# Pass 1 of an FFT and soft-MoE kernel: the last batch turned ahead of the remaining T, late T copies split between ScalarE and VectorE

## The chip, the core and the metric

One NeuronCore of a Trainium2 chip runs the whole program. The metric is device time in microseconds (us). Engines are named as in the profile: PE (TensorE, matrix multiply), PEld (its weight loads), DVE (VectorE), ACT (ScalarE), POOL (GpSimd), SP (SyncE, which issues nearly all DMAs).

## What is computed

```python
X = np.fft.fft(np.fft.fft(x, axis=1), axis=2).real   # x: 8 x 3072 x 256
x = X.reshape(24576, 256)
logits = x @ phi                                     # 32 slots
d = softmax over tokens;  c = softmax over slots
slot_out = experts(d.T @ x)                          # relu MLP, 8 experts
y = c @ slot_out
out = (s * relu(y @ w_in)**2 + b) @ w_out
```

The FFT is never formed. Pass 1, where the change lies, projects `x` on `phi` after a transform along the feature axis (folded into a small table `phd`), and then does the first of two steps of the transform along the sequence. Its result is the table `tt`, from which the next stage ("lp") makes the logits.

## The kernel before, in words

**Pass 1** (lines 357 to 481) has eight batches of three 1 MB pages of `x` each. A batch has two parts, so there are sixteen numbers n = 2b + part, and three kinds of step:

- V(n), `emit_v` (L371): matmuls (L383) of the pages of a part into the PSUM tile `vt`; part 0 needs the first two pages of its batch, part 1 the third. ScalarE copies `vt` to `vts` (L392).
- turn(n), `turn_v` (L394): TensorE transposes `vts` into `vq` (L401; four transposes in part 0, three in part 1). A copy (L405) takes `vq` to `v`; a planner's counter for each engine decides whether ScalarE or VectorE does it.
- T(b, h), `emit_t` (L413): for each half h of a batch four calls make 16 small matmuls (L422; 32 in the trace, where an f32 matmul has two records) into one PSUM tile `tps`, of which there are four buffers. The fourth call issues eight copies (L435) of the tile to `tt`, on ScalarE, or all eight on VectorE. T(b, .) needs the `v` of both parts of batch b.

The loop (L455) goes V(n), half a T (of the batch before), turn(n - 1). After the last V it runs T(6, 1), turn(15), and then, behind the last DMA issues of the pass, T(7, 0) and T(7, 1).

The program order of every engine is the order in which the Python code issues instructions. **The planner** (`at`, L107) is a set of counters, in us, for TensorE, ScalarE, VectorE and the DMA. `busy` adds a cost to a counter. `fill` (L138) issues steps of side work as long as VectorE's counter is not ahead of TensorE's. The side work of this pass is the loading, decoding and splitting of `w_out`: four loads of 1 MB (`raw`, L148), a chain on VectorE for each (L152 to L172, L198), at the end a maximum over partitions on TensorE (`mx`, L233 and L238), eight products on VectorE (L259), each with a cast on ScalarE (L261) and a subtraction on POOL (L262), and one matmul `bp` (L272) with its product on VectorE (L273). `pump_a` issues the loads in the order of a string (L289), in which the pages of `x` (x) and the loads of `w_out` (w) alternate; the first four pages go ahead of it. The third w lies between the two pages of part 0 of batch 4, the fourth between them and the third page of batch 5.

Behind pass 1, at L489 to L492, ScalarE fills a small constant `stack` with six instructions; its first use is much later (L815). Then comes the lp stage (L518): matmuls of `tt` with a table (L526), copies to `lg` on ScalarE (L539), maxima on VectorE (L541), a global maximum (L545 to L562), and then exponentials (L623). Much later the loads of `w2` (L762) go into pages that the experts' matmuls (L852) free.

Of the kernel before, what the change touches and what calls it, by code (L numbers as in the profile page):

```python
# [32 lines left out]
def tile_fft2__then__softmoe__then__act_relu2(  # L33
# [18 lines left out]
    nc = tc.nc  # L52
    P = 128
    NS1 = 24
    B, S, D = 8, NS1 * P, xp.shape[-1]
# [24 lines left out]
    ident = const.tile([P, P], F32, name="ident")  # L80
# [18 lines left out]
    def free_pages(among=9):  # L99
        return sum(max(p[1] - p[2], 0) for p in pools[:among])  # L100

    def drop(k):
        pools[k][2] -= 1

    todo = []
    side_work = []
# [7 lines left out]
    def busy(eng, cost, after=0.0):  # L114
        at[eng] = max(at[eng], after, at["pe"]) + cost
# [22 lines left out]
    def fill():  # L138
        while side_step(at["pe"] + 0.7):
            pass  # L140
# [44 lines left out]
    def keep_warm(t, k):  # L185

        for _ in range(k):
            nc.tensor.matmul(t, lhsT=ones[:, :t.shape[0]], rhs=ones[:, :t.shape[1]], start=True, stop=True)
# [117 lines left out]
    def pump_a():  # L306

        while order and at["dma"] < at["pe"] + LEAD and free_pages() >= (doubles[0][0] if order[0] == "w" else 1):
            order_step()

    x_at, pend_t, xr = [], [], []
# [33 lines left out]
    def htab_clear(i):  # L345
        for q in range(2):
            nc.gpsimd.memset(htabs[i][0][64 * q:64 * q + M, :, 1 - q], 0.0)
# [9 lines left out]
    with tc.tile_pool(name="xtp", bufs=1, side="right") as xtp, tc.tile_pool(name="vp", bufs=1, side="right") as vp, \  # L357
            tc.tile_pool(name="ps_v", bufs=1, space=PSUM) as psv:
        mxp[:] = [psv, 4]
        vs = [vp.tile([P, NE, NG * NR], F32, name=f"v{k}") for k in range(2)]  # L360
        for v in vs:
            nc.gpsimd.memset(v.rearrange("p e (b k) -> p e b k", b=NG)[:, :, :, NU:NR], 0.0)
        vts = {}

        def turned(n, c, i, k, rev):

            v = xa[n][0][:, c, i, P - 1:P] if rev else xa[n][0][:, c, i, 0:1]
            sg = -1 if rev else 1
            return bass.AP(tensor=v.tensor, offset=v.offset, ap=[list(v.ap[0]), [sg * 2 * P, k], [sg, P]])

        def emit_v(n):  # L371
            b, part = divmod(n, 2)
            x0, x2, x1 = 3 * b, 3 * b + 1, 3 * b + 2
            vt = psv.tile([P, 4, P], F32, name="vt", bufs=2)

            if part == 0:
                todo_v = [(0, 0, 0, x0, 0, 4, 0), (1, 0, 0, x0, 1, 4, 0), (0, 1, 1, x2, 6, 3, 1), (1, 1, 0, x2, 7, 4, 1)]
            else:
                todo_v = [(0, 0, 0, x1, 0, 3, 0), (1, 0, 0, x1, 1, 3, 0), (0, 1, 0, x2, 0, 1, 1), (1, 1, 0, x1, 7, 2, 1),
                          (0, 1, 1, x1, 6, 1, 1)]  # L380
            for c in range(2):
                for m, (h, sg, o, pg, i, k, rev) in enumerate(todo_v):
                    nc.tensor.matmul(vt[64 * h:64 * h + 64, o:o + k, :], lhsT=phd[:, c, sg, :],  # L383
                                     rhs=turned(pg, c, i, k, rev), start=(c == 0 and m < 2), stop=(c == 1 and m >= len(todo_v) - 2),
                                     tile_position=(0, 64 * h), skip_group_check=True)
            at["pe"] = max(at["pe"], x_at[x1 if part else x2]) + (2.3 if part else 3.6)
            for pg in ((x1, x2) if part else (x0,)):
                drop(xa[pg][1])
            busy("act", 0.5)
            ns = 3 if part else 4  # L390
            vts[n] = xtp.tile([P, 4, P], F32, name="vts", bufs=2)
            nc.scalar.copy(vts[n][:, 0:ns], vt[:, 0:ns])  # L392

        def turn_v(n):  # L394
            b, part = divmod(n, 2)
            bg, bq = divmod(b, NG)
            ns, nk = ((4, 16), (3, 10))[part]
            vq = psv.tile([P, 4, P], F32, name="vq", bufs=2)
            t = vts.pop(n)
            for si in range(ns):  # L400
                nc.tensor.transpose(vq[:, si, :], t[:, si, :], ident)  # L401
            at["pe"] += 0.44
            eng = "act" if at["act"] < at["dve"] + TOL else "dve"
            busy(eng, 0.65)
            (nc.scalar.copy if eng == "act" else nc.vector.tensor_copy)(  # L405
                vs[bg][:, :, NR * bq + 16 * part:NR * bq + 16 * part + nk],
                vq.rearrange("p s (k e) -> p e (s k)", e=NE)[:, :, 0:nk])
            if part:
                pend_t.extend((b, h) for h in range(2))

        part = []

        def emit_t():  # L413


            b, h = pend_t[0]
            bg, bq = divmod(b, NG)
            if not part:
                part[:] = [psv.tile([P, 4, P], F32, tag="tps", name="tps", bufs=4), 0]
            t, k = part  # L420
            for j in range(4):
                nc.tensor.matmul(t[32 * j:32 * j + 32, k, :], lhsT=vs[bg][:, 8 * j + 4 * h + k, NR * bq:NR * bq + NR],  # L422
                                 rhs=f_sb, start=True, stop=True, tile_position=(0, 32 * j), skip_group_check=True)
            at["pe"] += 0.3
            part[1] += 1
            if k < 3:
                return
            part.clear()
            pend_t.pop(0)
            eng = "dve" if h and not (side_work and b < B - 2) else "act"  # L430
            busy(eng, 3.4 if eng == "dve" else 3.0)
            for j in range(4):
                for c in range(2):
                    r = 64 * bg + NR * c
                    (nc.scalar.copy if eng == "act" else nc.vector.tensor_copy)(  # L435
                        tt[r:r + NR, :, bq, 8 * j + 4 * h:8 * j + 4 * h + 4],
                        t[NR * j:NR * j + NR, :, 64 * c:64 * c + 64].rearrange("p e k -> p k e"))

        def project():
            pp = psv.tile([P, 2, 2, NE], F32, tag="tps", name="pp", bufs=4)  # L440
            for j in range(2):
                for c in range(2):
                    for k in range(2):
                        nc.tensor.matmul(
                            pp[:, c, j, :], lhsT=dd[:, j, k, c * P:(c + 1) * P], rhs=phi_sb[:, k, :],
                            start=(k == 0), stop=(k == 1),
                        )
            for sg in range(2):
                nc.vector.tensor_copy(phd[:, :, sg], pp.rearrange("p c j e -> p c (j e)"))
            nc.vector.tensor_scalar(out=phd[:, :, 1, NE:], in0=pp[:, :, 1], scalar1=-1.0, scalar2=None, op0=ALU.mult)  # L450

        keep_warm(psv.tile([P, 4 * P], F32, tag="vt", name="warm", bufs=2)[:, :P], 7)
        project()
        NV = 2 * B
        for n in range(NV + 1):  # L455
            if n < NV:
                emit_v(n)
                pump_a()
                fill()
            if n == 3:  # L460
                tp = psv.tile([P, P], F32, tag="tps", name="tp", bufs=4)
                nc.tensor.transpose(tp, f_sb, ident)
                nc.vector.tensor_copy(ft_sb, tp)
            for _ in range(4):
                if pend_t:
                    emit_t()
            if n >= 1:
                turn_v(n - 1)
            fill()
            pump_a()  # L470
        while order:
            order_step()
        for _ in range(4):
            load_xr()
        while pend_t:
            emit_t()
        fill()
        for i in range(2):
            nc.gpsimd.tensor_copy(ltabs[i][0][64:P], ltabs[i][0][0:64])
        for i in range(2):  # L480
            htab_clear(i)
# [3 lines left out]
    stack = keep.tile([P, 2, 64], F32, name="stack")  # L485
    cmb = keep.tile([P, NE], F32, name="cmb")
    rm = keep.tile([R, 8, 16], F32, name="rm")
    si = keep.tile([P, 2, NE], F32, name="si")
    for h in (slice(0, 64), slice(64, P)):  # L489
        nc.scalar.copy(stack[h, 0, :], ident[h, h])  # L490
        nc.scalar.copy(stack[h, 1, 0:32], ident[h, h.start:h.start + 32])
        nc.scalar.mul(stack[h, 1, 32:64], ident[h, h.start + 32:h.stop], -1.0)  # L492


    lg = []
# [18 lines left out]
    with tc.tile_pool(name="ps_l", bufs=4, space=PSUM) as psl, \  # L514
# [3 lines left out]
        for st in range(NCH // 2 + SKEW):  # L518
            halves = [(h, st - SKEW * h) for h in range(2) if 0 <= st - SKEW * h < NCH // 2]
# [42 lines left out]
        nc.vector.tensor_copy(cmb, mb)  # L562
        mxp[0] = None
        keep_warm(warm, 8)

    temps.release()
    tpool.release()
# [375 lines left out]
    with tc.tile_pool(name="fr", bufs=4) as frp, tc.tile_pool(name="fo", bufs=3) as fo, \  # L943
# [27 lines left out]
        for r in range(4):  # L971
            eng = nc.vector.tensor_copy if r // 2 else nc.scalar.copy
# [194 lines left out]
```

## Time and profile before

| what | us |
|---|---|
| median of 3 runs | 1412.3 (1411.81 to 1413.08) |
| span of the profiled execution, first to last instruction | 1409.5 |
| what lies around the span (median less span) | 2.8 |
| PE busy in the span | 1379.2 (98%) |
| pass 1, up to the first matmul of lp | 98.5 |
| lp stage, up to the first exponential | 18.2 |

The profile comes from one execution; of its time only the span is shown, and the 2.8 us are the difference to the median of the three timed runs. Rows below give a start in us from the start of the span, then a duration. In the timeline, square brackets hold the idle time of the engine ahead of a row, and what ended it. In the chain of waits, each piece follows the one that released it.

### The profile page before, as it was taken

To read this page: it belongs to the slowest core of one execution; us is meant where nothing else is said; L and a number is where in the kernel's file an instruction comes from. 1 tells how busy PE (TensorE), PEld (TensorE's weight loads), DVE (VectorE), ACT (ScalarE), POOL (GpSimd) and SP (SyncE) were. 2 spreads that over 40 slices of the span, in tenths; PEclk is the share of its full clock that TensorE was granted. 3 is DMA by queue.
4 is the path that set the end of the run, shared out by engine and by line. 5 is a ranking of instruction groups with operands and counts; after the bars stand their busy time and mean duration, and the time that the engine had idled before them with its cause. 6 is when DMAs were issued, how large, how long until landed. Compare 5 with 4: busy or idle time off the path is not lost.

```text
span 1409.5 us, 23825 instructions
## 1 busy us (share of the span) xinstructions
PE 1379.2 (98%) x9314; PEld 836.7 (59%) x9314; DVE 1157.4 (82%) x1498; ACT 962.1 (68%) x1449; POOL 319.4 (23%) x298
## 2 busy tenths in 40 slices
PE   8978998999999999999999999999999999999998
PEld 5557554566666666666666666666666666666665
DVE  2667654998989898989898989898988888888885
ACT  2766213777777777777777777777777777777773
POOL 1243301521212121212121212121212121111110
PEclk9999999999999999999999999999999999999999
DMA  8996895101010101011010101010101010101000
GB/s 351 414 317 258 326 414 180 33 23 36 20 37 23 37 24 29 27 30 30 23 37 23 33 23 36 22 35 23 36 23 36 23 33 24 37 23 37 23 19 27
DMA packets 74528, 112.92 MB, mean 80 GB/s; under 512 B 35792, under 2 KB 61264, under 8 KB 67120
## 3 DMA queue, kind: packets, MB, share of 16 engines
q1 hardware_dynamic: 74288, 111.31, 22.9%
q8 instruction: 73, 1.20, 0.3%
q14 instruction: 39, 0.32, 0.1%
q0 software_dynamic: 128, 0.10, 0.0%
HBM read 78.48 MB, written 25.17 MB: 74 GB/s over the span
## 4 chain that ended last, share of the span: by engine, by line
PE 90%; DMA 4%; DVE 2%; ACT 1%; SPq 1%; POOL 0%; issue 0%; POOLq 0%; ACTq 0%
PE op L1027 46%; PE op L1029 23%; PE fhp L1000 11%; PE racc L681 3%; DMA xb<-in_x_turned_dram 3%; PE vt L383 2%; DMA w2t<-in_moe_w_dram 1%; PE dps L666 1%; PE tps L422 1%; DVE r L1005 1%; PE hp L606 1%; DVE cm L541 0%; POOL dt L586 0%; PE lp L526 0%; DVE rhl L991 0%
## 5 line engine op out<-in xcount | busy, mean ns | idle before, releaser
L1027 PE MATMUL op<-whl,rhl 128*128 128x512 f16 x3072 | 1025.9, 379 | 0.0
L1029 PE MATMUL op<-whl,rhl 128*128 128x256 f16 x3072 | 837.4, 273 | 0.3 <-DVE rhl L991 0.3
L1004 ACT ACTIVATE r<-fhp 128x768 f32<-128x768 f32 x512 | 413.2, 808 | 193.1 <-PE fhp L1000 190.2
L1005 DVE SCALAR_TENSOR_TENSOR r<-fhp,r 128x768 f32<-128x768 f32 x512 | 484.1, 949 | 24.3 <-ACT r L1004 22.5
L1027 PEld LDWEIGHTS <-rhl 128*128 128x128 f16 x3072 | 300.6, 98 | 335.2
L991 DVE TENSOR_TENSOR rhl<-r,rhl 128x768 f16<-128x768 f32 x500 | 489.7, 981 | 3.3 <-ACT rhl L990 0.9
L990 ACT CAST rhl<-r 128x768 f16<-128x768 f32 x508 | 420.2, 827 | 77.6 <-DVE r L1005 77.1
L1037 POOL TENSOR_TENSOR o<-o,bias 128x256 f32<-128x256 f32 x186 | 197.7, 1063 | 886.8 <-ACT o L1036 886.8
L1029 PEld LDWEIGHTS <-rhl 128*128 128x128 f16 x3072 | 300.6, 98 | 62.6 <-DVE rhl L991 0.7
L1000 PE MATMUL fhp<-ct,g 128*128 128x384 f16 x1024 | 249.9, 326 | 3.7 <-DVE r L1005 2.9
L1039 DVE SCALAR_TENSOR_TENSOR ot<-op,small,o 128x256 f32<-128x256 f32 x192 | 92.7, 483 | 104.6 <-POOL o L1037 104.4
L1000 PEld LDWEIGHTS <-g 128*128 128x128 f16 x1024 | 100.1, 98 | 71.2 <-issue 3.5
L1036 ACT ACTIVATE o<-op,small 128x256 f32<-128x256 f32 x186 | 88.2, 474 | 23.3 <-PE op L1029 22.6
L383 PE MATMUL vt<-xb,phd 128*64 128x512 f32 (+3 forms) x288 | 51.5, 489 | 7.1 <-DMA xb<-in_x_turned_dram 7.1
L681 PE MATMUL racc<-xrt,dh 128*64 128x256 f32 x384 | 44.3, 382 | 0.0
L435 ACT COPY tt<-tps 32x256 f32<-32x256 f32 x104 | 37.8, 363 | 7.6 <-PE tps L422 6.5
L383 PEld LDWEIGHTS vt<-xb,phd 128*64 128x64 f32 x288 | 25.2, 141 | 27.8 <-issue 18.1
L681 PEld LDWEIGHTS racc<-xrt,dh 128*64 128x64 f32 x384 | 26.4, 137 | 21.0 <-issue 6.0
L991 POOL TENSOR_TENSOR rhl<-r,rhl 128x768 f16<-128x768 f32 x12 | 20.2, 1701 | 55.8 <-DMA g<-gs 49.6
L392 ACT COPY vts<-vt 128x512 f32<-128x512 f32 (+1 forms) x16 | 8.5, 533 | 34.0 <-PE vt L383 33.8
L405 DVE COPY v<-vq 128x512 f32<-128x512 f32 (+1 forms) x13 | 8.0, 613 | 28.3 <-PE vq L401 28.3
L671 DVE COPY dh<-dps 128x512 f32<-128x512 f32 (+1 forms) x14 | 9.1, 651 | 20.0 <-PE dps L666 20.0
(212 smaller groups left out, 536.5 us busy)
## 6 DMA issues: line engine op xcount, KB each, us to landing
xb<-in_x_turned_dram SPq DMA_DIRECT2D x24, 1024.0 KB, 20.2
xrt<-in_x_pages_dram SPq DMA_DIRECT2D x24, 1024.0 KB, 10.8
out_dram<-ot SPq DMA_DIRECT2D x128, 128.0 KB, 1.7
w1t<-in_moe_w_dram SPq DMA_DIRECT2D x8, 1024.0 KB, 10.1
out_dram<-ot SPq DMA_DIRECT2D x128, 64.0 KB, 2.0
raw<-in_moe_w_out_dram SPq DMA_DIRECT2D x4, 1024.0 KB, 20.6
raw<-in_moe_w_in_dram SPq DMA_DIRECT2D x4, 1024.0 KB, 7.1
w2t<-in_moe_w_dram SPq DMA_DIRECT2D x4, 1024.0 KB, 12.1
```

The costliest lines, as they stand in the source:

```text
L383: nc.tensor.matmul(vt[64 * h:64 * h + 64, o:o + k, :], lhsT=phd[:, c, sg, :], rhs=turned(pg, c, i, k, rev), start=(c == 0 and m < 2), stop ...
L681: nc.tensor.matmul(raccs[acc][64 * h:64 * h + 64, :], lhsT=dh[:, m, g].rearrange("p j e -> p (j e)"), rhs=xr[k][0][:, g, t, :], start=(sum ...
L990: (nc.vector.tensor_copy if n < 2 and p % 4 == 2 else nc.scalar.copy)(a, r2)
L991: (nc.gpsimd if far else nc.vector).tensor_tensor(out=l, in0=r2, in1=a, op=ALU.subtract)
L1000: nc.tensor.matmul(hp[:, k, :].rearrange("p (s b m) -> p s b m", s=2, b=B), lhsT=g16[:, f * P:(f + 1) * P], rhs=c, start=True, stop=True)
L1004: nc.scalar.activation(out=r, in_=hp, func=AF.Relu, scale=1.0 / (CS * CS))
L1005: nc.vector.scalar_tensor_tensor(out=r2, in0=hp, scalar=0.0, in1=r, op0=ALU.max, op1=ALU.mult)
L1027: nc.tensor.matmul(op.rearrange("p h d -> p (h d)"), lhsT=a, rhs=w.rearrange("p h d -> p (h d)"), start=(f == 0), stop=False)
L1029: nc.tensor.matmul(op[:, 0, :], lhsT=l, rhs=w[:, 0, :], start=False, stop=(f == NFC - 1))
L1036: nc.scalar.activation(out=o1, in_=op[:, 1, :], func=AF.Copy, scale=qv)
L1037: nc.gpsimd.tensor_tensor(out=o1, in0=o1, in1=bias, op=ALU.add)
L1039: nc.vector.scalar_tensor_tensor(out=ot, in0=op[:, 0, :], scalar=qv, in1=o1, op0=ALU.mult, op1=ALU.add)
```

## The change

Within a batch, both V come first, then T of the batch before in both halves, then both turns. At the end V(14), T(6, 0), turn(14), V(15), turn(15) are followed by T(6, 1), T(7, 0) and T(7, 1). From batch 5 on, of the four pairs of copies of a half two go to VectorE and two to ScalarE; before batch 5 ScalarE does all. (Before, VectorE did all eight copies of the second half of a batch from batch 5 on.) The filling of `stack` moves behind the maxima of lp.

```diff
             part.clear()
             pend_t.pop(0)
-            eng = "dve" if h and not (side_work and b < B - 2) else "act"
-            busy(eng, 3.4 if eng == "dve" else 3.0)
             for j in range(4):
+                eng = "dve" if j % 2 and b >= B - 3 else "act"
+                busy(eng, 0.85 if eng == "dve" else 0.75)
                 for c in range(2):
...
-        NV = 2 * B
-        for n in range(NV + 1):
-            if n < NV:
-                emit_v(n)
-                pump_a()
-                fill()
-            if n == 3:
+
+        def step_v(n):
+            emit_v(n)
+            pump_a()
+            fill()
+
+        def step_t(halves):
+            for _ in range(4 * halves):
+                if pend_t:
+                    emit_t()
+
+        for b in range(B - 1):
+            step_v(2 * b)
+            step_v(2 * b + 1)
+            if b == 1:
                 tp = psv.tile([P, P], F32, tag="tps", name="tp", bufs=4)
                 nc.tensor.transpose(tp, f_sb, ident)
                 nc.vector.tensor_copy(ft_sb, tp)
-            for _ in range(4):
-                if pend_t:
-                    emit_t()
-            if n >= 1:
-                turn_v(n - 1)
+            step_t(2)
+            turn_v(2 * b)
+            turn_v(2 * b + 1)
             fill()
             pump_a()
+        step_v(2 * B - 2)
+        step_t(1)
+        turn_v(2 * B - 2)
+        step_v(2 * B - 1)
+        turn_v(2 * B - 1)
+        step_t(3)
         while order:
             order_step()
         for _ in range(4):
             load_xr()
-        while pend_t:
-            emit_t()
         fill()
...
-    for h in (slice(0, 64), slice(64, P)):
-        nc.scalar.copy(stack[h, 0, :], ident[h, h])
-        nc.scalar.copy(stack[h, 1, 0:32], ident[h, h.start:h.start + 32])
-        nc.scalar.mul(stack[h, 1, 32:64], ident[h, h.start + 32:h.stop], -1.0)
+
+    def fill_stack():
+        for h in (slice(0, 64), slice(64, P)):
+            nc.scalar.copy(stack[h, 0, :], ident[h, h])
+            nc.scalar.copy(stack[h, 1, 0:32], ident[h, h.start:h.start + 32])
+            nc.scalar.mul(stack[h, 1, 32:64], ident[h, h.start + 32:h.stop], -1.0)
...
         keep_warm(warm, 8)
+        fill_stack()
```

## Rows read from the trace of the kernel before

**Rows 1.** Head of the page

```profile
span 1409.5 us, 23825 instructions
```

**Rows 2.** Chain of waits, 52 to 99 us: start, duration, engine, tile, line

```profile
52.03 2.79 PE vt L383 x11
...
65.30 2.31 PE vt L383 x16
...
68.62 0.59 PE vq L401 x4
69.20 3.58 PE vt L383 x15
72.79 0.22 PE mx L233
...
73.74 1.01 PE tps L422 x32
74.75 0.48 PE vq L401 x3
...
79.13 0.43 PE bp L272 x2
...
91.03 0.43 ACT v L405
91.50 0.86 PE tps L422 x23
92.36 1.04 issue
...
97.96 0.55 issue
98.51 3.73 PE lp L526 x47
```

**Rows 3.** Timeline of DVE, 62 to 99 us

```profile
62.23 0.69 DVE L152 TENSOR_SCALAR wo<-raw 128x1024 uint32<-128x1024 uint32 x1 [1.27 <-DMA raw<-in_moe_w_out_dram]
...
69.24 0.69 DVE L405 COPY v<-vq 128x512 f32<-128x512 f32 x1 [0.38 <-PE vq L401]
...
75.26 0.49 DVE L405 COPY v<-vq 128x320 f32<-128x320 f32 x1 [0.35 <-PE vq L401]
75.67 3.79 DVE L259 TENSOR_SCALAR wo<-wo,small 128x512 f32<-128x512 f32 x7
...
79.98 0.47 DVE L273 TENSOR_SCALAR bias<-bp,sb_in 128x256 f32<-128x256 f32 x1
...
94.83 3.47 DVE L435 COPY tt<-tps 32x256 f32<-32x256 f32 x8 [1.74 <-PE tps L422]
```

**Rows 4.** Timeline of ACT, 87 to 117 us

```profile
87.05 0.48 ACT L392 COPY vts<-vt 128x384 f32<-128x384 f32 x1 [0.27 <-PE vt L383]
88.02 2.98 ACT L435 COPY tt<-tps 32x256 f32<-32x256 f32 x8 [0.49 <-PE tps L422]
...
96.96 0.24 ACT L490 COPY stack<-ident 64x64 f32<-64x64 f32 x1
...
102.23 2.20 ACT L539 COPY lg<-lp 112x512 f32<-112x512 f32 x4 [1.02 <-PE lp L526]
...
116.73 0.42 ACT L623 ACTIVATE dt<-dt 112x256 f32<-112x256 f32 x1 [1.97 <-DVE dt L586]
```

**Rows 5.** Stretches: length, then PE, PEld, DVE, ACT, POOL busy, clock, DMA share, GB/s

```profile
98.50:102.40 3.90, 3.89 (x57) 3.90 (x61) 0.69 (x1) 0.76 (x2) 0.00 (x0) 0.50 1.02 422
...
162.00:222.00 60.00, 56.98 (x512) 32.59 (x514) 33.83 (x46) 8.81 (x12) 0.75 (x1) 1.00 1.01 407
```

**Rows 6.** Stretches from the start, for the records of PE and PEld in them

```profile
0.00:97.00 97.00, 83.81 (x892) 51.50 (x892) 47.52 (x77) 53.06 (x133) 33.87 (x43) 0.99 0.98 356
...
0.00:112.25 112.25, 96.05 (x1148) 61.80 (x1148) 57.59 (x94) 61.67 (x153) 33.87 (x43) 0.97 0.98 364
```

**Rows 7.** DMA queues, 90.50 to 90.75 us: packets, MB, share of 16 engines

```profile
q8 instruction: 1, 0.02, 35.8%
```

## The prediction, made before the change was run

> **What bounds the kernel now.** I read the page first, for the span [rows 1], then the chain of waits [rows 2], and then the timelines of the engines that it names around pass 1. TensorE is the bound nearly everywhere; what can be won is idle time of TensorE on the chain. In pass 1 the chain waits for a page of x for the last time at 52.03 us, in V(8). From there to the end of V(15) it is TensorE alone, step behind step. Then it breaks: turn(15) is done at about 90.0, but its copy to `v` stands in ScalarE's queue behind the eight copies of T(6, 0) [rows 4] and runs at 91.03; T(7, 0) starts at 91.50, stops for 1.04 us at 92.36 for nothing that the profile shows, and T(7, 1) ends at 94.79. Its eight copies keep VectorE until 94.83 + 3.47 = 98.30 [rows 3]. The first lp matmul starts 0.21 us later, at 98.51. (The chain names `stack`, which ended 0.55 us before; VectorE's last copy is the nearer end.) So three things stand on the path: the wait for `v`, the gap of 1.04, and 3.47 of copies on one engine.
>
> **The change, part by part.**
>
> The new order of V, T and turns. The work of TensorE is the same: per batch 3.58 + 2.31 for the two V, 2 x 1.01 for T, 0.59 + 0.48 for the turns, 8.98 in all [rows 2]. What differs is when pages are needed. The second page of batch 4 lands at 52.0 [rows 2]; the fourth w lands at 62.2 [rows 3], four loads later, which is 2.55 us a load. So the third page of batch 4 is there at 54.6 and the third of batch 5, just behind the fourth w, at 64.8. Walk from 52.03: V(8) to 54.82, V(9) 57.13, T(3) 59.15, two turns 60.22, V(10) 63.80. V(11) waits for its page until 64.8 (a new wait of 1.0) and ends at 67.1. T(4) and turns 70.2, V(12) 73.8. `mx` takes 0.95 (72.79 to 73.74) [rows 2], 74.75; V(13) 77.05; `bp` 0.43, 77.5; T(5) and turns 80.6; V(14) 84.2. Later pages have slack: the second of batch 6 is there at 69.9, and V(12) starts at 70.2. Against the old order the new one has T(2, 1) and turn(7), 1.5 us, behind it by 52 us, in time in which it waited anyway; that pays for the new wait.
>
> VectorE ahead of T(6, 0). The side work now comes in this order on VectorE: eight products from about 75.4 (3.79 for seven, so 4.33), the product behind `bp` 0.47, to 80.2; then T(5)'s eight copies 3.47, to 83.7; then the copies for turn(12) and turn(13), 0.69 + 0.49, to 84.85 [rows 3]. T(6, 0) waits for the last of them, 0.65 us past 84.2. Which engine gets a copy to `v` I take from the planner's counters, added up in program order: turns 12, 13 and 15 go to VectorE, turn 14 to ScalarE. If the products run earlier, this wait is 0; if they slip by a further 1 us, it is 1.65.
>
> The tail. T(6, 0) 84.9 to 85.9, turn(14) to 86.5, V(15) to 88.8. The `vts` copy starts 0.11 later and takes 0.48 [rows 4], so turn(15) runs from 89.4 to 89.9, with 0.6 us of TensorE idle ahead of it, which is new. VectorE has `v` ready at 90.45, under T(6, 1), which ends at 90.9. T(7, 0) ends at 91.95, T(7, 1) at 92.95. The wait for `v` is gone, since no T copies stand ahead of this copy on its engine.
>
> The copies. Of T(6, 1), T(7, 0) and T(7, 1) VectorE has four each, twelve of 0.434 (3.47 / 8), 5.2 us from 90.95 on: 96.15. ScalarE's twelve take 12 x 0.373 (2.98 / 8) = 4.5 [rows 4] and end before. In total VectorE has 24 of these copies in either kernel. lp starts 0.2 behind: 96.35, against 98.51. That is 2.15 us won.
>
> The gap of 1.04 us. TensorE's instruction queue moves a packet at 90.5 [rows 7], lasting 0.358 x 0.25 x 16 = 1.43 us, just ahead of the gap. Two later packets of the queue, at 97.0 and 112.25, lie 2 x (1148 - 892) = 512 records apart [rows 6] with one packet between, so a block has 256 records. I estimate that a block is asked for when the one before is entered. Counting back 256 from the gap, that was in T(5, 1), at about 83.7; in the new order the same count lies early in V(14), at about 81. The packet could then come at about 88, and the gap would be 0; at the other end the packet still comes at 90.5 and TensorE goes on at 93.40. I take 0, since T(7, 0) may slip by 0.9 us before VectorE, busy with T(6, 1) until 92.7, notices. The Trainium skill (Runtime: NRT & Kernel Launch, Instruction fetch mechanics) has blocks of 256 instructions too, and says that crossing into the next is mostly hidden; the 1.04 us here were not, and by the rule alone the gap would be 0 in either kernel.
>
> `stack`. Its six instructions, 96.96 to 97.96 [rows 2, 4], were not the last end, so their going wins nothing now. In the new place they take 1.0 of ScalarE's 1.97 us of idle ahead of the first exponential [rows 4]. Without that cover the exponential would be 1.0 late.
>
> DMA issues. The string of loads is unchanged, and so is the order on SP; the four loads behind the pass now come after T in the program, which costs nothing, as the queue holds many earlier loads. POOL's subtractions follow ScalarE's casts and end some 8 us before lp.
>
> What becomes of the 2.15 us behind lp. Every stage up to the experts runs from TensorE and its helpers, so it moves as a whole. The DMA is full from 162 to 222 us [rows 5], but what starts its loads are pages that TensorE frees, which come earlier too. I count the gain in full.
>
> **The sum.** 1409.5 - 2.15 = 1407.35 of span; with the 2.8 that lie between this span and the median of 1412.3, 1410.15. Its own range: the wait ahead of T(6, 0) between 0 and 1.65 gives 1409.5 to 1411.15.
>
> **The rivals.**
>
> The clock stays up at the start of lp. TensorE is granted 0.50, the 1.2 GHz level, from 98.5 to 102.4 [rows 5], after it had done nothing from 94.79 on. The first two steps of lp took 98.51 to 102.23 [rows 2, 4], 3.72 us; at the 2.4 GHz level they take no less than half, so at most 1.86 would be won, and at least 0. I take 1.5 as the price, since the copy at the end doesn't depend on TensorE: 1408.65. For it: TensorE is idle for 3.4 us instead of 3.7, and before that it works without the old gaps, so the fall may come later than lp's first steps. Against it: 3.4 us are hardly less. The Trainium skill (TensorE: Matmul & The Clock Gate, What's actually happening) says that the low clock is the default, and that activity releases it; by that the clock falls in both kernels and this rival doesn't happen.
>
> The gap stays. The block lands at 93.40 as before. T(7, 0) ends at 93.8, VectorE's eight last copies take 3.47 to 97.3, and lp starts at 97.5: 1.0 won, 1411.3. For it: the packet moves while the DMAs carry many small packets, and they don't move with the change.
>
> The gain is lost to a transfer. If the loads of w2 ended no earlier, since the DMA is full for 60 us [rows 5], the time would stay at 1412.3. Against it: their start is released by TensorE.
>
> ScalarE becomes the bound, and it gets slower. All sixteen copies of a batch, 6.0 us, now stand ahead of the next `vts`. From the end of T(b, 0) until that `vts` is needed TensorE has 1.01 + 1.07 + 3.58 + 2.31 + 2.02 = 10.0 us of work; ScalarE needs 6.0 + 0.6, a margin of 3.4. It decides once ScalarE is later than that, by the casts of batches 5 and 6 or by slower copies; each of five batches that ran over by 1 us would cost 1: 1410.15 + 5 = 1415.15. Against it: 2.98 for eight copies is constant in the rows.
>
> **Chances and numbers.** The forecast 0.50, the clock 0.27, the gap 0.16, the transfer 0.03, ScalarE 0.04. A measurement of this kernel tells about 0.2% from no change, 2.8 us, so faster means below 1409.5. That takes nearly all of the clock's case (0.25) and the low edge of the forecast's (0.08): 0.33. Slower is ScalarE's case, 0.04. The same has the rest, 0.63. The range reaches from 1408.0, the clock's case with the wait ahead of T(6, 0) gone, to 1412.2, the gap's case with that wait at its longest; little but slow ScalarE and the lost transfer lies outside.
>
> **What the changed profile should show.** V(11) waits about 1 us for a page at 64. `v` for turn(15) is copied on VectorE, under T(6, 1). T(7, 1) ends near 93, VectorE's last `tt` copy near 96.2, and lp starts 0.2 later. VectorE still has 24 `tt` copies. The exponential doesn't wait for ScalarE. It would be wrong if lp started before 95 or after 97.5, if a `vts` copy made TensorE wait in batches 1 to 5, or if the time from lp's first matmul to the first exponential were not about 18.2 us.

## The result, and the profile after

| | before | after |
|---|---|---|
| median, us | 1412.3 (1411.38 to 1417.46, 5 runs) | 1421.03 (1419.72 to 1423.12, 5 runs) |
| after / before, 95% interval | | 1.006 (1.0042 to 1.0078) |
| profiled execution, us | about 1411.3 (estimate: its span and 1.8) | 1423.12 |
| its span, us | 1409.5 | 1421.3 |

The kernel became 8.7 us slower; 1410.15 was forecast, and the range ended at 1412.2. The changed kernel's profiled execution, the slowest of its five, took 1.8 us more than its span. The prediction put 2.8 around the span of before; with 1.8 the execution shown of before took about 1411.3, some 1 us under the median. The spans differ by 11.8, so the two executions lie further apart than the medians. Part of that is the start: the first page of x landed for V(0) at 13.36 instead of 10.77, and in the profiled executions of the experiments, with the same loads, between 11.4 and 13.2.

The loss lies ahead of lp. The first lp matmul starts at 109.61, not 98.51 [rows 2]: 11.1 later. From there to the end it is 1311.7, against 1311.0. Of the 11.1, 1.8 lie ahead of V(12), which starts at 72.01 instead of the 70.2 predicted, behind pages that came later; the rest is the 11.45 counted below, less the 2.15 that were forecast as won. The chain of waits of the changed kernel, with the same columns as [rows 2]:

```profile
76.61 2.31 PE vt L383 x17
...
81.51 2.70 DVE wo L259 x2
84.22 0.62 ACT whl L261
84.87 0.36 ACT tt L435
85.24 0.37 ACT tt L435
85.63 0.42 DVE tt L435
86.06 0.43 DVE tt L435
86.52 0.36 ACT tt L435
...
90.73 1.10 DVE v L405 x2
91.88 1.93 PE tps L422 x32
93.81 1.05 PE vq L401 x4
94.86 3.93 PE vt L383 x17
98.87 0.49 ACT vts L392
...
108.13 0.37 ACT tt L435
108.50 1.11 issue
109.61 5.51 PE lp L538 x77
```

Where [rows 2] had TensorE step behind step up to 90 us, the chain now leaves TensorE at 81.5 for VectorE's products (`wo`) and then goes back and forth between ScalarE and VectorE, copy by copy. T(5)'s sixteen copies last from 84.87 to the `v` copies at 90.73: 5.83 us with the last gap of 0.03 taken off. The prediction had them on two engines side by side, in 3.5. One behind the other they would be 8 x 0.373 + 8 x 0.434 = 6.5 us, and 5.83 is close to that.

The timeline of DVE, as [rows 3]:

```profile
77.30 6.89 DVE L259 TENSOR_SCALAR wo<-wo,small 128x512 f32<-128x512 f32 x8
...
85.63 0.85 DVE L435 COPY tt<-tps 32x256 f32<-32x256 f32 x2 [1.05 <-ACT tt L435]
...
90.73 1.09 DVE L405 COPY v<-vq 128x512 f32<-128x512 f32 x2
...
108.52 0.87 DVE L435 COPY tt<-tps 32x256 f32<-32x256 f32 x2 [0.80 <-ACT tt L435]
```

Two things are new. VectorE starts its `tt` copies only when a `tt` copy of ScalarE has ended, though both read a `tps` tile that TensorE has finished, and they write different rows. And the eight products take 6.89 us where the prediction had 4.33. The view of waits adds the first up, in both directions (total in us, times, longest):

```profile
DVE tt L435 <- ACT tt L435: 10.0, 9, 2.8
...
ACT tt L435 <- DVE tt L435: 5.9, 6, 1.1
```

The timeline of PE shows what this does to TensorE:

```profile
66.91 2.37 PE L383 MATMUL vt<-xb,phd 128*64 128x384 f32 x20 [1.42 <-DMA xb<-in_x_turned_dram]
...
72.01 3.65 PE L383 MATMUL vt<-xb,phd 128*64 128x512 f32 x16
...
91.88 1.93 PE L422 MATMUL tps<-f_sb,v 128*32 128x128 f32 x32 [5.95 <-DVE v L405]
...
99.40 0.55 PE L401 MATMUL vq<-ident,vts 128*128 128x128 f32 x3 [0.64 <-ACT vts L392]
```

T(6, 0) waits 5.95 us for `v`, where 0.65 was predicted, and then takes 1.93 instead of 1.01 [rows 2]. The windows say why (length, then PE, PEld, DVE, ACT, POOL busy, clock, DMA share, GB/s):

```profile
85.90:91.80 5.90, 0.03 (x1) 0.00 (x0) 4.20 (x10) 2.75 (x7) 4.59 (x5) 0.95 0.97 203
91.80:97.00 5.20, 5.12 (x48) 3.51 (x50) 1.55 (x5) 2.03 (x5) 4.25 (x5) 0.50 1.01 267
109.60:114.00 4.40, 4.39 (x68) 4.40 (x72) 0.76 (x2) 1.27 (x3) 0.00 (x0) 0.50 1.01 419
```

TensorE did nothing for 5.9 us, and in the 5.2 us behind that its granted clock is 0.50, the 1.2 GHz level: T(6, 0), turn(14) and most of V(15) run at half speed. At the start of lp it is 0.50 as before [rows 5].

From the start of V(12) to that of lp the prediction had 96.35 - 70.2 = 26.15 us; measured were 109.61 - 72.01 = 37.60. The 11.45 between them split by the rows into three:

| stretch | predicted | measured | more |
|---|---|---|---|
| V(12) starts to T(6, 0) starts | 14.65 | 19.87 | 5.2 |
| T(6, 0) starts to T(6, 1) ends (clock 0.50 at first) | 6.05 | 9.1 | 3.1 |
| T(6, 1) ends to lp starts (last copies) | 5.45 | 8.6 | 3.2 |

The 5.2 of the first line split once more: products and the one behind `bp` end at 84.58, 2.57 later against V(12) than predicted; the copies take 5.83 instead of 3.47, 2.36 more; 0.29 lie between.

Why did the products get slower? The rows of L259 by source line, first before, then after in two stretches, up to 78.5 and from 79.0 (count, then least, median and most ns, and the first and last start):

```profile
L259 DVE TENSOR_SCALAR wo<-wo,small x8: 474/476/1408, 74.4 to 79.0; 128x512 f32<-128x512 f32 x8
```

```profile
L259 DVE TENSOR_SCALAR wo<-wo,small x4: 483/483/487, 77.3 to 78.5; 128x512 f32<-128x512 f32 x4
...
L259 DVE TENSOR_SCALAR wo<-wo,small x4: 1380/1386/1392, 78.9 to 82.8; 128x512 f32<-128x512 f32 x4
```

The same instruction at its least takes 0.48 us in both. Before, one of the eight took 1.41; now the last four take 1.38 to 1.39 each. The timelines show who works beside them. Before, POOL and then DVE around the slow one, then the rest of POOL's subtractions; behind it POOL after:

```profile
75.64 1.16 POOL L262 TENSOR_TENSOR whl<-wo,whl 128x512 f16<-128x512 f32 x1 [3.49 <-ACT whl L261]
75.67 1.41 DVE L259 TENSOR_SCALAR wo<-wo,small 128x512 f32<-128x512 f32 x1
...
79.29 7.90 POOL L262 TENSOR_TENSOR whl<-wo,whl 128x512 f16<-128x512 f32 x7 [2.49 <-ACT whl L261]
```

```profile
78.57 9.97 POOL L262 TENSOR_TENSOR whl<-wo,whl 128x512 f16<-128x512 f32 x8 [2.92 <-issue]
```

Before, the first subtraction ran beside the second product, and the other seven began when the products were over (the last started at 79.0): T(4, 1)'s eight copies stood on ScalarE from 75.59 on, for 2.98 us, ahead of the casts that the subtractions need. In the new order T(4) is earlier, ScalarE casts each product as it comes, and POOL subtracts beside VectorE's next products. The Trainium skill (SBUF — State Buffer, Who interferes with whom) says that VectorE and GpSimd have one pair of ports in common, and that where an instruction of VectorE uses it too, whichever comes first holds it for the whole instruction. The rows agree: the slow product of before ends at 77.08, 0.28 us behind the end of the subtraction at 76.80, and in the trace of after each of the four ends 0.28 to 0.29 behind one. An experiment below takes the overlap away.

### The profile page after: what moved, and what is told of

The parts are those of the page before. It is cut to its first block, busy times and chain, and to the rows that moved or that the text cites. A ratio compares the mean times of both kernels' runs of the same rounds, so it can differ in the third digit from the quotient of the medians.

```text
span 1421.3 us, 23827 instructions
## 1 busy us (share of the span) xinstructions
PE 1381.3 (97%) x9314; PEld 840.8 (59%) x9314; DVE 1160.4 (82%) x1499; ACT 962.6 (68%) x1448; POOL 320.8 (23%) x298
## 4 chain that ended last, share of the span: by engine, by line
PE 89%; DMA 5%; DVE 3%; ACT 1%; SPq 1%; issue 1%; POOL 0%; POOLq 0%; ACTq 0%
PE op L1040 46%; PE op L1042 23%; PE fhp L1013 11%; DMA xb<-in_x_turned_dram 4%; PE racc L694 3%; DMA w2t<-in_moe_w_dram 1%; PE vt L383 1%; PE dps L679 1%; DVE r L1018 1%; PE hp L619 1%; PE lp L538 1%; PE tps L422 0%; POOL dt L599 0%; DVE tt L435 0%; DVE rhl L1004 0%
```

## Experiments

The theory: (A) ScalarE and VectorE take turns on a `tps` tile, so a half shared by both is no quicker, and slower than two halves on one engine each; (B) POOL's subtractions beside the products slow those; (C) the clock falls because of the wait that A and B make. The rival: the new order of V, T and turns is itself the cause. Ratios are to the kernel before in the same series (medians 1412.3 for the change, 1413.05 for e1 to e4, 1413.32 for e5 to e10 and 1412.48 for e11 and e12).

| kernel | median, us | ratio (95%) | V(12) to T(6, 0) | V(12) to lp |
|---|---|---|---|---|
| before | | | | 29.38, old |
| the change | 1421.03 | 1.006 (1.0042 to 1.0078) | 19.87 | 37.60 |
| e1, one engine a half | 1417.34 | 1.0032 (1.0021 to 1.0043) | 16.93 | 31.92 |
| e2, split alone | 1420.01 | 1.0042 (1.0023 to 1.006) | | 36.02, old |
| e3, two tiles | 1418.04 | 1.0033 (1.0022 to 1.0044) | | 31.41 |
| e4, POOL later | 1419.96 | 1.0048 (1.003 to 1.0066) | 17.65 | 35.37 |
| e5, e1 and e4 | 1413.23 | 1.0003 (0.9993 to 1.0012) | 14.13 | 27.61 |
| e7, e5 and last half shared | 1411.36 | 0.9989 (0.9978 to 1.0) | | 25.91 |
| e8, tail alone | 1411.92 | 0.9998 (0.9989 to 1.0007) | | 26.54, old |
| e10, `stack` alone | 1412.38 | 0.9997 (0.9985 to 1.001) | | 28.27, old |
| e11, e7 with its tail filled | 1409.93 | 0.9988 (0.9976 to 1.0001) | | 25.49 |
| e12, e8 with one tile | 1413.9 | 1.0008 (0.9999 to 1.0017) | | 30.78, old |

The last two columns are stretches in us by the timelines of PE, in one profiled execution each. In the old order T(4, 1) and turn(11), 1.49 us of TensorE [rows 2], lie behind V(12) too. So the stretches marked old have that much more work in them; less the 1.49, before has 27.89.

**e1: the changed kernel, each half of T copied by one engine, by the old rule.**

```
-                eng = "dve" if j % 2 and b >= B - 3 else "act"
-                busy(eng, 0.85 if eng == "dve" else 0.75)
+            eng = "dve" if h and not (side_work and b < B - 2) else "act"
+            busy(eng, 3.4 if eng == "dve" else 3.0)
```

> The new order of V, T and turns, with the copies of a half on one engine as before (first halves ScalarE, second halves of the late batches VectorE). Theory S (ScalarE and VectorE do not read one PSUM tile at the same time, so the split puts their copies one behind the other): batch 5's sixteen copies take 3.5 us instead of 5.8, T(6, 0) starts 3 us sooner, the tail's copies end after 7.0 instead of 8.4 us, TensorE's clock falls less; lp starts about 7 us sooner, time 1412.5 to 1416. Rival O (the order itself costs the time, whatever the engines): 1419 to 1422. Rival D (the split runs side by side and the loss is VectorE's side work alone): slower than the changed kernel by about 2 us, 1423.

The DVE timeline has T(5, 1)'s copies in a row and without a wait:

```profile
83.80 3.47 DVE L435 COPY tt<-tps 32x256 f32<-32x256 f32 x8
```

The PE timeline:

```profile
88.14 1.09 PE L422 MATMUL tps<-f_sb,v 128*32 128x128 f32 x32 [3.01 <-DVE v L405]
...
103.13 7.29 PE L538 MATMUL lp<-tt,ltab 64*64 64x128 f32 x114 [5.49 <-issue]
```

T(6, 0) comes 19.87 - 16.93 = 2.94 us sooner, and lp 5.7. The rest of the wait, 3.01, stands behind the slow products, which are unchanged at 6.89. Behind this shorter wait the clock falls later and for less: T(6, 0) takes 1.09, and V(15) 3.49, where it is 3.97 in the change and 2.38 in e5. Sharing the copies cost time, and it isn't the whole loss: 1417.34 lies above the 1412.5 to 1416 that theory A alone had expected.

**e2: the kernel before, with the split of the copies alone.**

```
-            eng = "dve" if h and not (side_work and b < B - 2) else "act"
-            busy(eng, 3.4 if eng == "dve" else 3.0)
+                eng = "dve" if j % 2 and b >= B - 3 else "act"
+                busy(eng, 0.85 if eng == "dve" else 0.75)
```

> The kernel before with the split of the late copies alone. Theory S: each of the six late halves takes 3.4 us of both engines in turn; T(6, 0) waits for v(13) until about 89.8, the copies end about 104.5, lp starts 6 us later than before: 1416 to 1420. Rival O: the split is harmless or helps, 1410.5 to 1412.5, as the last eight copies would end 1 us sooner. Rival D: as O.

In the old order, without anything else of the change, the split loses some 6 us, and lp starts 36.02 us after V(12) instead of 29.38. The waits of 60 to 115 us:

```profile
DVE tt L435 <- ACT tt L435: 14.0, 10, 4.2
```

and its PE timeline, where lp starts at 106.20:

```profile
106.20 5.50 PE L526 MATMUL lp<-tt,ltab 64*64 64x128 f32 x82 [4.73 <-ACT stack L492]
```

So A holds in either order, and the rival can't be the whole cause.

**e3: the changed kernel, each engine's quarters in a `tps` tile of their own** (from batch 5 on).

```
-                part[:] = [psv.tile([P, 4, P], F32, tag="tps", name="tps", bufs=4), 0]
+                two = [psv.tile([P, 4, P], F32, tag="tps", name="tps", bufs=4) for _ in range(2 if b >= B - 3 else 1)]
+                part[:] = [two, 0]
...
+                t = two[j % len(two)]
```

> The changed kernel, where from batch 5 on the two ScalarE quarters of a half and the two VectorE quarters lie in PSUM tiles of their own (two of the four buffers). Theory S: the copies run side by side, batch 5's in 3.5 us, the tail's in about 5.2 to 6; T(6, 0) starts 2.6 us sooner and lp about 6 to 8.5 us sooner: 1412.5 to 1415.5. If instead the two engines hinder each other in PSUM whatever the tile, nothing changes: 1420 to 1422. Rival O: 1419 to 1422.

The timelines of DVE and then of ACT have T(5)'s copies side by side:

```profile
83.84 3.49 DVE L437 COPY tt<-tps 32x256 f32<-32x256 f32 x8
...
97.21 5.26 DVE L437 COPY tt<-tps 32x256 f32<-32x256 f32 x12 [0.57 <-PE tps L424]
```

```profile
84.10 2.98 ACT L437 COPY tt<-tps 32x256 f32<-32x256 f32 x8
```

That is the prediction's picture: eight and eight copies in 3.5 us, and twelve of the tail in 5.26, where 5.2 was predicted. The only difference to the change is the tile, so it is the tile that the engines take turns on. The time is no better than e1's because the second tile takes a buffer. PE's timeline has the new wait:

```profile
83.87 1.50 PE L424 MATMUL tps<-f_sb,v 128*32 128x128 f32 x30 [3.85 <-DVE bias L273]
```

T(5, 1) waits 3.85 us for a `tps` buffer that `bp` holds until VectorE has its product, behind the slow eight. With this wait and the slow products left, 1418.04 misses the 1412.5 to 1415.5 expected.

The Trainium skill (PSUM — Partial Sum Buffer, PSUM bank collisions raise a hardware error) says that two engines' accesses to one bank must be kept apart where they meet in the same quarter of the partitions, and that guarding by bank is the simple version of this. The quarters here lie on different partitions, so by that rule they might be read at once; the semaphores of the program hold them apart by tile all the same, and whether the reads could overlap on the chip was not tried.

**e4: the changed kernel, POOL's subtractions held until the products are done.**

```
-        nc.gpsimd.tensor_tensor(out=whl[h][:, k, 1, :], in0=wo[h][:, k], in1=whl[h][:, k, 0, :], op=ALU.subtract)
+        late_sub.append(lambda: nc.gpsimd.tensor_tensor(
+            out=whl[h][:, k, 1, :], in0=wo[h][:, k], in1=whl[h][:, k, 0, :], op=ALU.subtract))
...
+        nc.gpsimd.tensor_copy(small[:, 20:21], bias[:, 0:1])
+        for f in late_sub:
+            f()
```

> The changed kernel, with POOL's eight subtractions of the split of w_out held until VectorE's eight products are done (a small POOL copy that reads what VectorE writes after them stands ahead). Theory P (a product slows from 0.48 to about 0.9 to 1.4 us while POOL runs): the products take 4.3 instead of 6.9 us, T(6, 0) starts 2.5 us sooner, 1417.5 to 1419.5, and the copies still alternate. Rival (POOL does not matter): products 6.9, 1420 to 1422.

The rows of the products, then the DVE timeline:

```profile
L261 DVE TENSOR_SCALAR wo<-wo,small x8: 478/480/487, 78.7 to 81.5; 128x512 f32<-128x512 f32 x8
```

```profile
78.68 3.26 DVE L261 TENSOR_SCALAR wo<-wo,small 128x512 f32<-128x512 f32 x8
```

Every product takes 0.48 us again, eight 3.26 instead of 6.89, and T(6, 0) starts 2.22 sooner after V(12). The copies still take turns, so it still waits, and at half the clock:

```profile
91.03 1.94 PE L428 MATMUL tps<-f_sb,v 128*32 128x128 f32 x32 [3.72 <-DVE v L411]
```

B holds, at the smaller share. The two medians, 1419.96 (1417.5 to 1419.5 expected) and 1421.03, alone wouldn't tell e4 from the change; the rows do.

**e5: e4 with the edit of e1 as well.** The new order stays, with both causes gone.

```
-                eng = "dve" if j % 2 and b >= B - 3 else "act"
-                busy(eng, 0.85 if eng == "dve" else 0.75)
+            eng = "dve" if h and not (side_work and b < B - 2) else "act"
+            busy(eng, 3.4 if eng == "dve" else 3.0)
```

> The new order with one engine for each half, and POOL's subtractions held until the products are done. Theory S + P (the order itself is harmless; the losses are the copies in turn and the products slowed by POOL): products 3.3 to 4.3 us, v for T(6, 0) is ready before V(14) ends, so that TensorE does not wait there (3.0 us with one engine alone), and lp starts near 99: 1412.5 to 1414.5, equal to the kernel before. Rival O (about 4 us belong to the order whatever the engines do): 1416 to 1418.

The PE timeline:

```profile
87.21 1.08 PE L428 MATMUL tps<-f_sb,v 128*32 128x128 f32 x32 [0.20 <-ACT v L411]
...
100.69 5.56 PE L544 MATMUL lp<-tt,ltab 64*64 64x128 f32 x81 [5.49 <-DMA xrt<-in_x_pages_dram]
```

T(6, 0) waits 0.20 us, and takes 1.08: the granted clock is 1.00 in each of the windows of 4 us from 84 to 96 in this execution. V(12) to T(6, 0) is 14.13, against 14.65 predicted. The whole loss is gone (ratio 1.0003), so the rival falls: the order costs nothing beyond 0.12%. And C holds: without the wait there is no half clock. But there is no gain either: lp starts 27.61 after V(12), since T(6, 1)'s and T(7, 1)'s sixteen copies stand on VectorE alone, by its timeline:

```profile
93.52 6.96 DVE L441 COPY tt<-tps 32x256 f32<-32x256 f32 x16 [0.55 <-PE tps L428]
```

**e7: e5, with only the last half, T(7, 1), shared, in two tiles.**

```
+                two = [psv.tile([P, 4, P], F32, tag="tps", name="tps", bufs=4) for _ in range(2 if (b, h) == (B - 1, 1) else 1)]
...
+                if late:
+                    eng = "dve" if j % 2 else "act"
```

> As the kernel with one engine for each half and POOL held, but the very last half, T(7, 1), lies in two PSUM tiles, one for each engine. Theory S: its copies take 1.74 instead of 3.47 us behind VectorE's copies of T(6, 1), lp starts 1.7 us sooner than in that kernel: 1410.5 to 1413. If sharing over two tiles does not help: as that kernel.

V(12) to lp is 25.91, under the 26.15 predicted; the ratio is 0.9989, with 1.0 at the end of its interval. **e11** fills what was left of the idle time: T(6, 1) stands ahead of turn(15) again, and of T(7, 1)'s quarters ScalarE has one and VectorE three.

```
+        step_t(1)
...
-        step_t(3)
+        step_t(2)
```

> The new order, one engine for each half, POOL held, and in the tail T(6, 1) ahead of turn(15), with T(7, 1) in two tiles: one quarter on ScalarE, three on VectorE. Theory: the 0.7 us in which TensorE waits for vts(15) is filled, VectorE starts T(6, 1)'s copies 1.2 us sooner; V(12) to lp takes 25.3 to 25.8 us (25.9 with T(7, 1) shared by halves): 1410.5 to 1412, at or a little below that kernel's 1411.4. If ScalarE's T(7, 0) bounds the end: as that kernel.

The timelines of PE and of DVE:

```profile
96.26 4.72 PE L550 MATMUL lp<-tt,ltab 64*64 64x128 f32 x82 [3.43 <-DMA xrt<-in_x_pages_dram]
```

```profile
89.95 6.09 DVE L446 COPY tt<-tps 32x256 f32<-32x256 f32 x14 [2.66 <-PE tps L430]
```

lp starts 25.49 after V(12). VectorE's last copy ends at 96.04, and the page of x that lp waits for by its row landed at 95.84 by the chain, so mending the copies further would soon win nothing. 1409.93 is the lowest median of all. Its interval reaches 1.0001, so a gain of about 0.1% is likely and not shown.

**e8 and e12: the kernel before, with its own tail mended,** turn(15) ahead of T(6, 1) and T(7, 1) shared, in e8 on two tiles, in e12 on one.

```
+            if n == NV:
+                turn_v(n - 1)
...
-            if n >= 1:
+            if 1 <= n < NV:
                 turn_v(n - 1)
...
+                    eng = "dve" if j % 2 else "act"
```

> The kernel before, with only its tail changed: turn(15) ahead of T(6, 1), its v on VectorE, and T(7, 1) in two PSUM tiles, one for each engine. Theory: v(15) no longer waits behind eight copies on ScalarE (1 us), the last half's copies take 1.74 instead of 3.47 us; lp starts 2 to 2.7 us sooner than before: 1409.5 to 1411.5 beside 1412.3 to 1413. Rival (T(7, 0) runs into the instruction fetch at 93.4 all the same): half of that or less, 1411.5 to 1413.

and from e8 to e12

```
-                two = [psv.tile([P, 4, P], F32, tag="tps", name="tps", bufs=4) for _ in range(2 if (b, h) == (B - 1, 1) else 1)]
+                two = [psv.tile([P, 4, P], F32, tag="tps", name="tps", bufs=4) for _ in range(1)]
```

> The old order with its tail changed, as in the earlier run, but T(7, 1)'s copies, shared by the two engines, read one PSUM tile. Theory S: ScalarE's part starts behind T(7, 0), and the two engines take turns, 3.3 us instead of 1.7; V(12) to lp takes 28 to 28.7 us against 26.5 with two tiles, 1.5 to 2 us more: 1413 to 1414.5. Rival (the tile does not matter): as with two tiles, 1411.5 to 1412.5.

On two tiles (e8's timelines of DVE and ACT) both engines run through:

```profile
92.96 5.22 DVE L440 COPY tt<-tps 32x256 f32<-32x256 f32 x12 [0.28 <-PE tps L424]
```

```profile
91.04 7.47 ACT L440 COPY tt<-tps 32x256 f32<-32x256 f32 x20 [0.49 <-PE tps L424]
```

On one tile (e12's timeline of DVE) they stop for each other:

```profile
97.92 0.85 DVE L440 COPY tt<-tps 32x256 f32<-32x256 f32 x2 [3.75 <-ACT tt L440]
99.57 0.87 DVE L440 COPY tt<-tps 32x256 f32<-32x256 f32 x2 [0.80 <-ACT tt L440]
```

V(12) to lp is 26.54 in e8 and 30.78 in e12. Not all of the 4.2 is the tile: T(7, 0) of e12 stands behind a stop of 2.31 us that waits for nothing the row names (the last section comes back to it):

```profile
93.64 1.69 PE L424 MATMUL tps<-f_sb,v 128*32 128x128 f32 x41 [2.31 <-issue]
```

The rest, 1.9 us, is mostly what the turns cost in the eight copies of T(7, 1): 3.3 (97.15 to 100.44) instead of 4 x 0.434 = 1.7. Against the kernel before, e8's time can't be told apart, and 1411.92 lies just above the 1409.5 to 1411.5 expected. But less the 1.49 its stretch is 25.05, against 27.89 before: lp starts no later behind V(12) than in e7 and e11, in the old order. No run shows that the new order adds anything to that.

**e10: the kernel before, with only `stack` filled later.**

> The kernel before with the filling of stack moved alone. Theory: its 1.0 us on ScalarE was not the last end, and the new place has cover: no change, 1412 to 1413.5. Rival (lp did wait for it): 0.2 to 1 us faster at the start of lp.

```
+        fill_stack()
```

Ratio 0.9997: nothing. ScalarE's idle time ahead of the first exponential is 1.08 us instead of 1.97 [rows 4], so the cover held, in the changed kernel too (1.08).

## Why the prediction was wrong

**What failed: the copies.** "Of T(6, 1), T(7, 0) and T(7, 1) VectorE has four each, twelve of 0.434, 5.2 us", with ScalarE's twelve beside them; and "T(5)'s eight copies 3.47". Both count the engines as independent. They read one tile, and the program lets one in at a time: 5.83 instead of 3.47, and 8.6 from the end of T(6, 1) to lp instead of 5.45. e2 shows it by itself, and e3 gives the predicted durations back by a second tile. A sign of it stood in the trace of before, and the prediction doesn't use it: in its waits VectorE's maximum of the lp sums, another reader of a PSUM tile that ScalarE copies, waits for that copy.

```profile
DVE cm L541 <- ACT lg L539: 5.2, 4, 2.9
```

**What failed: the products.** "Eight products from about 75.4 (3.79 for seven, so 4.33)" took the duration from the old order, in which POOL's subtractions came behind them. The change moved what keeps ScalarE busy, and so when POOL starts. The term measured 6.89, and 3.26 where POOL waits (e4). The row of seven held a sign of this too: 3.79 has the one product of 1.41 in it that ran beside the one early subtraction, which the prediction spread over all eight. The bounds of the wait ahead of T(6, 0), 0 to 1.65, let the products slip by 1 us only; 5.95 was measured. e1 and e4 give 2.9 and 2.2 us of it back, e5 all but 0.20.

**What was missing: the clock behind that wait.** The sum has no term for it, since a wait of 0.65 makes none; at 5.95 it cost 3.1 us more. That the clock falls behind such a wait stood in the rows of before [rows 5], where 3.7 us of idle time came ahead of lp, and the prediction prices it there alone.

**The rivals.** The clock at lp's start was 0.50 as forecast, and the gap at T(7, 0) was gone. The rival that ended slower had ScalarE late behind sixteen copies in batches 1 to 5. That didn't happen: the waits have no `vts` copy ahead of TensorE but the one at turn(15), 0.64, where 0.6 was predicted. The time came out on that rival's side by another mechanism, and lp started at 109.61, far behind the 97.5 that the prediction gave as its sign of being wrong.

**What was right.** V(11) waits for its page until 66.9, for 1.42 (1.0 predicted). In the new order TensorE's other steps stand as walked, and e5 has V(12) to T(6, 0) in 14.13 against 14.65. `stack` costs nothing. What happens at lp moves the whole rest: from the first lp matmul to the first exponential it is 128.33 - 109.61 = 18.72 (18.22 before), and the end follows within 0.7; over all twelve profiles it lies 1310.5 to 1312.6 behind lp's start. With A and B removed and the last half in two tiles, e7 and e11 start lp 25.91 and 25.49 after V(12), where 26.15 was predicted. Their ratios of 0.9989 and 0.9988 are near the 0.9985 of the forecast (1410.15 / 1412.3), with 1 inside or at the end of their intervals. So lp can start as early as was counted. But the order alone doesn't do it: e5 has the order and starts lp 27.61 after V(12), 0.3 sooner than the 27.89 of before, and e8 reaches 25.05 in the old order. The gain is in the tail, and the copies as the change makes them throw it away, and more.

## What to carry to other kernels

Before copies of one PSUM tile are shared by two engines, look in the trace for a wait of the one on the other's read of the same tile; where there is one, give each engine a tile of its own and ask which buffer that takes away (e3's 3.85 us). When a step is moved, ask of every engine behind it what will now run at the same time, since a duration read from the old order holds for the old neighbours: here a product went from 0.48 to 1.39 us. Look at the single rows behind such a sum: one product of 1.41 in the old order showed the price. And TensorE's wait of 5.95 us was paid twice, once as idle time and once in steps at half the clock behind it.

## What the runs showed of the hardware that wasn't expected

- VectorE's product of 128 x 512 takes 0.48 us alone and 1.37 to 1.41 where it starts beside one of POOL's subtractions; with POOL held back all eight took 0.478 to 0.487. In the changed kernel the subtractions slow as well, from 1.15 alone to 1.34 to 1.42 beside products.
- The `tt` copies aren't slowed by the same subtractions: in e5, where these run from 82.39 to 91.38, the eight on VectorE from 82.57 on take 3.47, as alone [rows 3].
- `tt` copies kept their durations when both engines worked at the same time on two tiles: 3.49 for eight on VectorE and 2.98 on ScalarE, as alone [rows 3, 4]. What costs is the wait, not the reading.
- The stop of TensorE that the prediction put down to its instruction queue was 1.04 us before [rows 2], 2.31 in e12, and absent in e10, which has the order of before. Before and in e12 it stands at the same place, behind 851 matmul records by the views of stretches. By the DMA queues, the instruction queue's packet ends at about 92.05 in both, and TensorE goes on 1.4 and 1.6 us later. In e10 the packet ends at about 88.9, some 6 us before TensorE comes to that place. In the changed kernel it starts at 87.8, where the prediction had about 88, and ends while TensorE waits anyway. So the stop goes with a late packet, as the prediction took it; why the packet comes 3 us later in some executions stays open.
